# Dynamic convolution and a max-out layer on one core: one earlier tap addition, a gate by transfer, sums in three parts, one logarithm a group later

## The chip, the cores and the metric

One core of a Trainium2 chip runs the whole program. The metric is the time of the execution on the device in microseconds (us), lower is better. Times of before are medians of three runs; the profile is that of one further execution of the same kernel.

## The reference, cut to what matters

Input `x` has 8 sequences of 4160 rows of 192 channels in 8 heads; `weight_gen` gives, for each row and head, 7 logits. Then:

```
w   = exp(weight_gen - max) / sum(exp(...))             # softmax over the 7 taps
out[s] = sum over k of w[s, head, k] * x[s - 6 + k]      # 7 taps, zeros ahead of each sequence
h1, h2 = out @ w1, out @ w2                              # 192 -> 1024 twice
result = maximum(h1, h2) @ w_out                         # 1024 -> 192
```

The kernel writes `maximum(h1, h2)` as `h1 + relu(h2 - h1)`, so TensorE computes one hidden layer with `w2 - w1` (tile `wd`), ScalarE applies the relu, and the part `out @ w1 @ w_out` is one small product with a matrix worked out once (tile `w10`). The softmax goes without the maximum: exponential, sum of seven, logarithm of the sum, subtraction, exponential.

## The kernel before, in words

The 33280 rows are laid out as 128 partitions by 260 columns. **Batches** of 16 columns (17 of them, 0 to 16; the last two have 12 and 8) go through the softmax and the taps; **units** of 8 columns (4 in batches 0 and 1 and at the very end) go through the products. Columns 24 to 27 are the unit of batch 1 at offset 8, unit 6. For each batch, in this order:

- **ScalarE** `X` (`exp_sum`, line 153): exponentials of all logits, tile `e_t`.
- **VectorE** `red` (line 168): sums of seven, tile `sum_t`. `part` splits a batch into `of` parts by columns.
- **ScalarE** `l` (`ln`, line 172): the logarithm of all the sums of a batch in one instruction; it so waits for the last part of `red`.
- **VectorE** `shift` (line 177): logits minus logarithm, in three parts.
- **ScalarE** `W` (`weights`, line 191): the exponentials of that, the softmax weights, per half batch.
- **VectorE** `mul` (line 211): seven products per element, tile `m_t`; `adds`: three additions (lines 227, 233, 236) that bring seven taps to one, tile `y_t`. The second reads what the first wrote, and the third what the second wrote. A hook, `beside`, is called ahead of each of the three and places the parts of `shift` (first half of a batch) or of `red` (second half, two batches ahead of the one multiplied) between them. In the second half `red` takes two parts, ahead of the first and the second addition; nothing stands between the second and the third.
- **SyncE** turns `y_t` to `yt` by a transposing DMA (line 245). **GpSimd** then reads one column of `yt` into the tile `gate` (line 253); as its queue is in order, the loads of `x` and `weight_gen` behind it (lines 118, 125, 139) start only when the transpose has landed.

In batches 0 and 1 the seven taps are not added on VectorE: TensorE adds them while it transposes (`sum_transpose`, line 281; steps `y.0` to `y.7`), 7 taps by 6 blocks by 2 halves, 84 matmuls for a unit. These steps, and all others of the first 47 us, stand in a list written out by hand, `OPENING`: `m.1.8` is the product for columns 24 to 27, `s.2` the shift of batch 2 behind it, `W.2.0` the weights that wait for that.

From tile 16 on, **groups** of three tiles (`hidden`, groups 8 and up) repeat one order. TensorE: hidden products into the PSUM tiles `hda` and `hdb` (line 336); the first half of an output group (lines 388, 376, tile `op_ps`); hidden product into `hdc`; the second half of the outputs. ScalarE, in order: relu of `hda` and of `hdb` (line 346), steps listed as "before" (place 0), relu of `hdc`, evacuation of `op_ps` (line 434), steps listed as "after" (place 1). Each of the four PSUM tiles has one buffer: TensorE writes `hda` of the next group when the relu of this one has read it, and `op_ps` when it has been evacuated. `SOFTMAX_AT` gives for each group and place the steps `X`, `l` and `W`: the logarithm of batch 5 is "after" group 16, that of batch 10 "after" group 44, those of 8, 12 and 15 are "before".

VectorE's steps hang on the tile number (`extra`) and run in their order, without a place among the groups; transposes follow as they are done. At the end ScalarE copies the last two columns to `o_last` (line 422) and two queues store them.

Of the kernel before, what the change touches and what calls it, by code (L numbers as in the profile page):

```python
# [9 lines left out]
FP32 = mybir.dt.float32  # L10
BF16 = mybir.dt.bfloat16
# [6 lines left out]
def _sub(base: bass.AP, off: int, dims):  # L18
    ap = [list(base.ap[0])] + [[int(s), int(c)] for s, c in dims]
    return dataclasses.replace(base, offset=base.offset + off, ap=ap)  # L20
# [3 lines left out]
def kernel(  # L24
# [9 lines left out]
    nc = tc.nc  # L34

    B, S, D = x.shape
    H, K = weight_gen.shape[2], weight_gen.shape[3]
    F = moe_w1.shape[1]
    P = 128
# [3 lines left out]
    HF = F // 2  # L43
# [120 lines left out]
    def red(b, i=0, of=1):  # L164
        if i == 0:
            s_ts[b] = psm.tile([P, BATCHES[b][1] * H], FP32, name="sum_t", tag="sum")
        hs, at, ap = part(b, i, of)
        nc.vector.reduce_sum(out=s_ts[b][:, hs], in_=_sub(e_ts[b], at, ap), axis=AX.X)  # L168
# [48 lines left out]
    def adds(b, o, first=False, beside=lambda i, of: None):  # L217


        w = dict(pieces(b))[o]  # L220
        n = w * D

        def taps(at, step, cnt):
            return _sub(m_t, K * o * D + at * n, [[step * n, cnt], [1, w * D]])

        beside(0, 3)
        nc.vector.tensor_tensor(out=taps(0, 1, 3), in0=taps(0, 1, 3), in1=taps(3, 1, 3), op=ALU.add)  # L227
        if first:
            return
        beside(1, 3)  # L230
        if b not in y_ts:
            y_ts[b] = py.tile([P, 16 * D], BF16, name="y_t", tag="y")
        nc.vector.tensor_tensor(out=taps(0, 2, 2), in0=taps(0, 2, 2), in1=taps(1, 5, 2), op=ALU.add)  # L233
        beside(2, 3)

        nc.vector.tensor_tensor(  # L236
            out=_sub(y_ts[b], o * D, [[64, 2], [P, 3 * w // 2], [1, 64]]),
            in0=taps(0, 1, 1), in1=taps(2, 1, 1), op=ALU.add,
        )

    def transpose(u):

        b, o, n = UNITS[u]
        yt = pyt.tile([P, 8 // 2 * 3 * P], BF16, name="yt", tag="yt")
        nc.sync.dma_start_transpose(
            out=yt[:, 0:n // 2 * 3 * P].rearrange("p (b t) -> p b t", t=P),
            in_=y_ts[b][:, o * D:(o + n) * D],
        )
        yt_ts[u] = yt
        while held:  # L250
            held.pop(0)()

        nc.gpsimd.tensor_copy(out=gate, in_=yt[:, 0:1])  # L253
        c = b + 1 if o == 0 else b + 2
        if u == 8:
            load_x(c, 0, 8)
        if o == 8 and c < NB:
            load_x(c, 0, min(8, BATCHES[c][1]))
        if o == 0 and c < NB and BATCHES[c][1] > 8:
            load_x(c, 8, BATCHES[c][1] - 8)  # L260
        if o == 0 and b + 3 < NB:
            load_wg(b + 3, nc.gpsimd)
# [2 lines left out]
        return slice(64 * j, 64 * j + 64)  # L265


    LEFT = (0, 1, 2, K - 1)

    def sum_transpose(u, i=None):  # L270

        b, o, n = UNITS[u]
        assert n == 4
        to = "h" if i == 0 else "o"
        yps = yps_of[u, i] = ps[to].tile([P, 1024], FP32, name="yps", tag="hd" if i == 0 else "op")
        ks = range(6) if i is None else range(3 * i, 3 * i + 3)
        for k in ks:
            for t in range(K):
                at = K * o * D + (t * 6 + k if i is None else (K * i + t) * 3 + k % 3) * P
                for r in range(2):  # L280
                    nc.tensor.matmul(  # L281
                        yps[:, r * 512 + k * 64:r * 512 + (k + 1) * 64],
                        lhsT=m_t[half(r), at:at + P], rhs=ident[half(r), half(r)],
                        start=(k == ks[0] and t == 0), stop=(t == K - 1),
                        skip_group_check=True,
                    )
# [129 lines left out]
    def evac(p, n):  # L416

        tile_, at = op_at[p]
        o = o_t[0]
        if p == NT // 2 - 1:  # L420

            nc.scalar.copy(out=_sub(o_last, 0, [[D, 2], [1, D]]),
                           in_=_sub(tile_, at, [[512, 2], [1, D]]))
            for j, eng in enumerate((nc.scalar, nc.sync)):
                eng.dma_start(
                    out=bass.AP(tensor=out.tensor, offset=dcol(place(p)[0] + 2 * j) * D, ap=[[CPP * D, P], [1, D]]),
                    in_=o_last[:, j * D:(j + 1) * D],
                )
            return
        runs = [[q for q in range(p, p + n) if column(2 * q)[0] == u]  # L430
                for u in range(column(2 * p)[0], column(2 * (p + n - 1))[0] + 1)]
        for qs in runs:
            c, h = place(qs[0])
            copied = nc.scalar.copy(out=_sub(o, c % 24 * D, [[D, len(qs)], [h * D, 2], [1, D]]),  # L434
                           in_=_sub(tile_, at + (qs[0] - p) * D, [[D, len(qs)], [512, 2], [1, D]]))
        stores = []
        for q in range(p, p + n):
            u, i, _ = column(2 * q)
            if u == NU - 2 and UNITS[u][2] == 8 and i % 2:
                stores.append((nc.sync, place(q)[0] - 1, [4 * D, 2], [1, 2 * D]))  # L440
            elif u < NU - 1 and i == UNITS[u][2] // 2 - 1:
                w = i + 1
                for k in range(0, 2 * w, w if u in PARTED else 2 * w):
                    stores.append((nc.sync, place(q)[0] - i + k, [1, (w if u in PARTED else 2 * w) * D]))
            if u == NU - 1:
                stores.append((nc.sync, place(q)[0], [2 * D, 2], [1, D]))
        for eng, c, *ap in stores:

            def issue(eng=eng, c=c, ap=ap, o=o):
                eng.dma_start(  # L450
                    out=bass.AP(tensor=out.tensor, offset=dcol(c) * D, ap=[[CPP * D, P], *ap]),
                    in_=_sub(o, c % 24 * D, ap),
                )

            if 3 <= u < NU - 3:
                held.append(issue)
            else:
                while u > 3 and held:
                    held.pop(0)()
                issue()  # L460
        return copied
# [80 lines left out]
    around = consts.tile([P, 2 * P], BF16, name="around")  # L542
    ident, swap = around[:, 0:P], around[:, 64:64 + P]
    zeros = consts.tile([P, PAD * D], BF16, name="zeros")
    gate = consts.tile([P, 1], FP32, name="gate")
    o_last = consts.tile([P, 2 * D], FP32, name="o_last")

    pstage = ctx.enter_context(ExitStack())
    stage = pstage.enter_context(tc.tile_pool(name="pstage", bufs=1))
# [13 lines left out]
    def load_w(h, wi):  # L563

        wsrc = (moe_w1, moe_w2)[wi]
        return nc.sync.dma_start(
            out=ws["E", wi][:, h * HF:(h + 1) * HF],
            in_=bass.AP(tensor=wsrc.tensor, offset=h * HF, ap=[[F, P], [1, HF]]),
        )

    def load_last(h, wi):

        wsrc = (moe_w1, moe_w2)[wi]
        return nc.sync.dma_start(  # L574
            out=ws["T", wi][half(h), :],
            in_=bass.AP(tensor=wsrc.tensor, offset=P * F + h * HF, ap=[[F, 64], [1, HF]]),
        )
# [124 lines left out]
    def results_buffer(_):  # L702
# [22 lines left out]
        e.0.1 d.0 d.2 t.0 k.3 t.2 T.3 d.1 T.4 h.0 h.1 t.1 X.1 r.0 lx.0.8.4 T.1 lo.0 r.1 m.0.4 n.1 v.0 h.2  # L725
        lx.1.0.8 V.1 y.1 r.2 l.1 h.3 e.1 m.0.8 lg.2@l.1 s.1 V.0 m.0.12 r.3 h.4 W.1.0 m.1.0 y.2 h.5 r.4 p.0
        e.2 r.5 h.6 lx.1.8.8@r.4 lg.3@e.2 y.3 W.1.8 h.7 lh.2 C.1 C.0 C.2 A.3 W.1.4 X.2 r.6 e.3 B.3 m.1.4 h.8
        D.3 y.4 r.7 r.8 Z.0 E.3 n.2 X.3 l.2 m.1.8 A.4 e.4 W.1.12 lx.2.0.8.0@r.7 B.4 h.9 D.4 h.10 r.9 E.4 s.2
        r.10 lg.4@r.9 y.5 W.2.0 A.5 h.11 B.5 h.12 e.5 D.5 n.3 r.11 r.12 A.6 m.1.12 E.5 h.13 B.6 D.6 y.6 r.13
        E.6 h.14 e.6 l.3 lx.2.8.8@r.13 h.15 r.14 A.7 W.2.8 B.7 y.7 D.7 r.15 e.7 E.7  # L730
    """

    make_identity(nc, ident_f)
# [3 lines left out]
    for step in OPENING.split():  # L737
# [4 lines left out]
            behind(act_of[after], act_of[step])  # L742

    SOFTMAX_AT = {
        (9, 1): "X.4 W.3.0", (12, 0): "W.3.8 l.4", (14, 1): "X.5", (16, 0): "W.4.0", (16, 1): "l.5",
        (18, 1): "W.4.8", (19, 0): "X.6", (21, 1): "W.5.0", (23, 1): "W.5.8 l.6", (25, 1): "X.7",
        (27, 1): "W.6.0", (29, 0): "l.7", (29, 1): "W.6.8 X.8", (33, 1): "W.7.0", (34, 0): "l.8",
        (35, 1): "W.7.8", (37, 1): "X.9 W.8.0", (39, 1): "W.8.8", (40, 0): "l.9", (41, 1): "X.10",
# [13 lines left out]
    def extra(t):  # L762

        u, k = TILES[t]
        b, o, n = UNITS[u]
        s = o + k

        if s == 0 and b + 1 < NB:
            mul(b + 1, 0)
        later = 0 if b < 4 else 5  # L770
        if s == later and b + 1 < NB:

            c = b + 1
            adds(c, 0, beside=lambda i, of: shift(c + 1, i, of) if c + 1 < NB else None)
        if s == 8 and b + 2 < NB:
            mul(b + 1, 8)
        if s == 8 + later and b + 2 < NB:
            adds(b + 1, 8, beside=lambda i, of: red(b + 3, i, 2) if b + 3 < NB and i < 2 else None)
        if s == 8 and b + 2 == NB:
            mul(b + 1, 4)  # L780
            adds(b + 1, 4)
        if k == n // 4 - 1 and 7 < u + 1 < NU:
            transpose(u + 1)
# [41 lines left out]
```

## Time and profile before

| | us |
|---|---|
| median of three runs | 405.51 (405.4 to 405.52) |
| profiled execution, its own time | 405.37 |
| its span in the trace | 403.6 |
| TensorE matmul busy | 394.8 |
| VectorE busy | 369.1 |
| ScalarE busy | 360.9 |
| GpSimd busy | 72.3 |
| granted TensorE clock | 1.0 of full speed |

The span is the time from the first to the last instruction or transfer of the trace; 1.77 us of the execution's own time lie around it. A row of the timeline has the start, the busy time, the engine, the line, the operation with its output and inputs, and in brackets the idle time before it with what ended it. A busy time includes the end of the pipeline, so the next instruction of an engine may start up to 0.1 us ahead of the end of the one before: what an instruction costs in a row of others is the distance of two starts, not its busy time.

### The profile page before, as it was taken

How to read it: one execution, taken by the hardware profiler on the slowest of the kernel's cores; microseconds unless marked ns; L12 is line 12 of the kernel's file. 1: busy time of each engine (PE TensorE's matmuls, PEld its weight loads, DVE VectorE, ACT ScalarE, POOL GpSimd, SP SyncE). 2: the span in 40 equal slices, each digit the busy share in tenths (PEclk: the TensorE clock that was granted, in tenths of full speed). 3: DMA queues.
4: the chain of work that ended last, by engine and by line, in shares of the span. 5: the costliest groups of instructions: out<-in, count | busy, mean ns of one | idle time of the engine just before them, and what ended most of it. 6: DMA issues, size and time to landing. Idle time of an engine off the chain costs nothing.

```text
span 403.6 us, 16321 instructions
## 1 busy us (share of the span) xinstructions
PE 394.8 (98%) x7499; PEld 321.3 (80%) x7499; DVE 369.1 (91%) x211; ACT 360.9 (89%) x466; POOL 72.3 (18%) x96
## 2 busy tenths in 40 slices
PE   7799999999999999999999999999999999999996
PEld 3589999777778777778777778877777877787996
DVE  5999999999999999999999999999999999998200
ACT  5999899999999989999899999989999899888872
POOL 3111031211122210222220122122012121200000
PEclk9999999999999999999999999999999999999999
DMA  8956468767768646864766667777457847558304
GB/s 262 222 140 151 120 124 167 183 164 133 190 110 222 182 79 129 240 187 80 217 187 107 141 192 193 99 215 198 81 115 228 178 80 200 141 106 193 104 31 169
DMA packets 60883, 63.16 MB, mean 157 GB/s; under 512 B 47641, under 2 KB 48665, under 8 KB 60816
## 3 DMA queue, kind: packets, MB, share of 16 engines
q1 hardware_dynamic: 52816, 40.15, 36.4%
q0 software_dynamic: 7856, 21.89, 27.4%
q8 instruction: 58, 0.95, 1.0%
q10 hardware_dynamic: 144, 0.10, 0.1%
q14 instruction: 9, 0.07, 0.1%
HBM read 36.55 MB, written 25.56 MB: 154 GB/s over the span
## 4 chain that ended last, share of the span: by engine, by line
PE 92%; ACT 5%; DMA 1%; SPq 1%; issue 0%
PE op_ps L376 42%; PE hdc L336 13%; PE hdb L336 13%; PE hda L336 13%; PE op_ps L388 8%; ACT rd_t L346 2%; DMA ws0E<-in_moe_w_dram 1%; PE hdp L336 1%; PE yps L281 1%; ACT en_t L191 1%; ACT yt L293 1%; ACT e_t L153 0%; ACT w1t L644 0%; SPq L574 0%; ACT w L622 0%
## 5 line engine op out<-in xcount | busy, mean ns | idle before, releaser
L376 PE MATMUL op_ps<-wo,rd_t 64*128 64x192 bf16 x4160 | 210.6, 243 | 0.0
L376 PEld LDWEIGHTS <-rd_t 64*128 64x128 bf16 x4160 | 181.0, 94 | 14.7
L211 DVE TENSOR_TENSOR m_t<-xb,en_t 128x10752 bf16<-128x10752 bf16 (+2 forms) x39 | 187.8, 4821 | 1.5 <-ACT en_t L191 1.4
L336 PEld LDWEIGHTS <-wd 64*128 64x128 bf16 x1824 | 96.8, 94 | 40.4 <-issue 2.5
L346 ACT ACTIVATE rd_t<-hdc 128x1024 bf16<-128x1024 f32 x82 | 84.1, 1025 | 17.8 <-PE hdc L336 16.2
L253 POOL CAST gate<-yt 128x1 f32<-128x1 bf16 x30 | 39.9, 1332 | 271.3 <-DMA yt<-y_t 271.3
L346 ACT ACTIVATE rd_t<-hda 128x1024 bf16<-128x1024 f32 x81 | 83.4, 1030 | 0.2 <-ACT o_t L434 0.2
L346 ACT ACTIVATE rd_t<-hdb 128x1024 bf16<-128x1024 f32 x81 | 83.5, 1031 | 0.0
L227 DVE TENSOR_TENSOR m_t<-m_t 128x4608 bf16<-128x4608 bf16 (+1 forms) x30 | 73.0, 2433 | 0.1
L336 PE MATMUL hdc<-yt,wd 64*128 64x512 bf16 (+1 forms) x552 | 67.9, 353 | 0.0
L434 ACT COPY o_t<-op_ps 128x384 f32<-128x384 f32 (+1 forms) x99 | 56.1, 577 | 12.4 <-PE op_ps L376 12.3
L336 PE MATMUL hdb<-yt,wd 64*128 64x512 bf16 (+1 forms) x540 | 67.1, 355 | 0.0
L336 PE MATMUL hda<-yt,wd 64*128 64x512 bf16 (+1 forms) x540 | 67.1, 355 | 0.0
L388 PE MATMUL op_ps<-w,yt 64*128 64x192 bf16 x780 | 55.5, 243 | 0.0
L388 PEld LDWEIGHTS <-yt 64*128 64x128 bf16 x780 | 39.0, 94 | 14.5 <-issue 0.3
L233 DVE TENSOR_TENSOR m_t<-m_t 128x3072 bf16<-128x3072 bf16 (+1 forms) x30 | 50.2, 1674 | 0.1
L191 ACT ACTIVATE en_t<-wg_t 128x896 bf16<-128x896 f32 (+3 forms) x48 | 35.7, 773 | 3.0 <-PE op_ps L376 2.0
L236 DVE TENSOR_TENSOR y_t<-m_t 128x1536 bf16<-128x1536 bf16 (+1 forms) x30 | 27.5, 916 | 0.6
L177 DVE TENSOR_TENSOR wg_t<-wg_t,sum_t 128x280 f32<-128x280 f32 (+6 forms) x46 | 22.2, 483 | 0.0
L168 DVE TENSOR_REDUCE sum_t<-e_t 128x64 f32<-128x448 f32 (+3 forms) x31 | 19.7, 639 | 2.3 <-ACT e_t L153 2.3
L125 POOL DMA_DIRECT2D xb<-in_x_dram x34 | 18.2, 537 | 17.3 <-ACT rd_t L346 11.0
L153 ACT ACTIVATE e_t<-wg_t 128x896 f32<-128x896 f32 (+2 forms) x18 | 15.9, 886 | 2.1 <-DMA wg_t<-in_weight_gen_dram 2.1
(40 smaller groups left out, 110.0 us busy)
## 6 DMA issues: line engine op xcount, KB each, us to landing
out_dram<-o_t SPq DMA_DIRECT2D x21, 768.0 KB, 4.3
xb<-in_x_dram POOLq DMA_DIRECT2D x30, 384.0 KB, 5.0
out_dram<-o_t SPq DMA_DIRECT2D x22, 384.0 KB, 3.7
wg_t<-in_weight_gen_dram POOLq DMA_DIRECT2D x13, 448.0 KB, 5.7
xb<-xb POOLq DMA_DIRECT2D x7, 288.0 KB, 5.1
wg_t<-in_weight_gen_dram SPq DMA_DIRECT2D x2, 448.0 KB, 5.2
xb<-in_x_dram POOLq DMA_DIRECT2D x4, 192.0 KB, 6.4
xs<-in_x_dram SPq DMA_DIRECT2D x1, 576.0 KB, 4.3
```

The costliest lines, as they stand in the source:

```text
L177: nc.vector.tensor_tensor(out=w_t, in0=w_t, in1=_sub(s_ts[b], hs.start, [[1, hs.stop - hs.start], [0, K]]), op=ALU.subtract)
L191: act = nc.scalar.activation(out=_sub(en_ts[b], (o * WGC + ((i or 0) * J + j) * N * K) * 2, [[2 * N, K], [2, N], [1, 2]]), in_=_sub(wg_ts[ ...
L211: return nc.vector.tensor_tensor(out=m_out, in0=x_in, in1=_sub(en_ts[b], at * H * 2, [[2, K * n * H], [0, G // 2], [1, 2]]), op=ALU.mult,)
L227: nc.vector.tensor_tensor(out=taps(0, 1, 3), in0=taps(0, 1, 3), in1=taps(3, 1, 3), op=ALU.add)
L233: nc.vector.tensor_tensor(out=taps(0, 2, 2), in0=taps(0, 2, 2), in1=taps(1, 5, 2), op=ALU.add)
L236: nc.vector.tensor_tensor(out=_sub(y_ts[b], o * D, [[64, 2], [P, 3 * w // 2], [1, 64]]), in0=taps(0, 1, 1), in1=taps(2, 1, 1), op=ALU.add,)
L253: nc.gpsimd.tensor_copy(out=gate, in_=yt[:, 0:1])
L336: nc.tensor.matmul(hid_out(t, f, j), lhsT=wd_at(j, s, f // 4, f % 4 * P, P), rhs=_sub(yt_ts[u][half(j), :], (s + j) % 3 * P, [[3 * P, w // ...
L346: relu_of[t0] = nc.scalar.activation(out=rd[:, k * 1024:(k + n) * 1024], in_=hd[:, at:at + n * 1024], func=AF.Relu)
L376: return nc.tensor.matmul(op_out(c), lhsT=rd[rows, k * 1024 + at:k * 1024 + at + P], rhs=wo[rows, f * D:(f + 1) * D], start=False, stop=(r ...
L388: nc.tensor.matmul(op_out(c + j), lhsT=yt_ts[u][half(j), (3 * i + (s + j) % 3) * P:(3 * i + (s + j) % 3 + 1) * P], rhs=w10[half(j), s * D: ...
L434: copied = nc.scalar.copy(out=_sub(o, c % 24 * D, [[D, len(qs)], [h * D, 2], [1, D]]), in_=_sub(tile_, at + (qs[0] - p) * D, [[D, len(qs)] ...
```

## The change

Five edits that act, and two that do not:

1. `OPENING` has a new step `a.1.8` right behind `m.1.8`: VectorE adds taps 3, 4, 5 to taps 0, 1, 2 of columns 24 to 27 (the first of the three additions, 128x2304). `sum_transpose` of that unit then goes over taps 0, 1, 2 and 6: 48 matmuls in place of 84.
2. `gate` is filled by a DMA on GpSimd's queue that reads two elements of `yt`, in place of a copy by GpSimd of 128 elements.
3. The sums of batches 4 to 16 take three parts in place of two; the third stands between the second and the third addition.
4. The logarithm of batch 5 moves from "after" group 16 to "after" group 17. All others keep their places.
5. At the very end `o_last` is two tiles of one column each. ScalarE copies one and its queue stores it; VectorE copies the other and SyncE's queue stores it.

`load_w` and `load_last` get new cases which no step uses, and an unused constant goes. All other steps, their engines and their order are as before.

```diff
         nc.vector.tensor_tensor(out=taps(0, 1, 3), in0=taps(0, 1, 3), in1=taps(3, 1, 3), op=ALU.add)
         if first:
+            fewer.add((b, o))
             return
...
-        nc.gpsimd.tensor_copy(out=gate, in_=yt[:, 0:1])
+        nc.gpsimd.dma_start(out=gate, in_=yt[0:1, 0:2])
...
+        taps = (0, 1, 2, K - 1) if (b, o) in fewer else range(K)
         for k in ks:
-            for t in range(K):
+            for t in taps:
...
-            nc.scalar.copy(out=_sub(o_last, 0, [[D, 2], [1, D]]),
-                           in_=_sub(tile_, at, [[512, 2], [1, D]]))
-            for j, eng in enumerate((nc.scalar, nc.sync)):
+            for j, (eng, copy) in enumerate(((nc.scalar, nc.scalar.copy), (nc.sync, nc.vector.tensor_copy))):
+                copy(out=o_last[j], in_=tile_[:, at + 512 * j:at + 512 * j + D])
...
-        D.3 y.4 r.7 r.8 Z.0 E.3 n.2 X.3 l.2 m.1.8 A.4 e.4 W.1.12 lx.2.0.8.0@r.7 B.4 h.9 D.4 h.10 r.9 E.4 s.2
-        r.10 lg.4@r.9 y.5 W.2.0 A.5 h.11 B.5 h.12 e.5 D.5 n.3 r.11 r.12 A.6 m.1.12 E.5 h.13 B.6 D.6 y.6 r.13
+        D.3 y.4 r.7 r.8 Z.0 E.3 n.2 X.3 l.2 m.1.8 a.1.8 A.4 e.4 W.1.12 lx.2.0.8.0@r.7 B.4 h.9 D.4 h.10 r.9
+        E.4 s.2 r.10 lg.4@r.9 y.5 W.2.0 A.5 h.11 B.5 h.12 e.5 D.5 n.3 r.11 r.12 A.6 m.1.12 E.5 h.13 B.6 D.6
...
-        (9, 1): "X.4 W.3.0", (12, 0): "W.3.8 l.4", (14, 1): "X.5", (16, 0): "W.4.0", (16, 1): "l.5",
+        (9, 1): "X.4 W.3.0", (12, 0): "W.3.8 l.4", (14, 1): "X.5", (16, 0): "W.4.0", (17, 1): "l.5",
...
-            adds(b + 1, 8, beside=lambda i, of: red(b + 3, i, 2) if b + 3 < NB and i < 2 else None)
+            adds(b + 1, 8, beside=lambda i, of: red(b + 3, i, 3) if b + 3 < NB else None)
```

## The prediction

> **What bounds the kernel now.** I read the head of the page first, then the chain that ended last, then the costliest groups.
>
> ```profile
> span 403.6 us, 16321 instructions
> PE 394.8 (98%) x7499; PEld 321.3 (80%) x7499; DVE 369.1 (91%) x211; ACT 360.9 (89%) x466; POOL 72.3 (18%) x96
> PE 92%; ACT 5%; DMA 1%; SPq 1%; issue 0%
> L211 DVE TENSOR_TENSOR m_t<-xb,en_t 128x10752 bf16<-128x10752 bf16 (+2 forms) x39 | 187.8, 4821 | 1.5 <-ACT en_t L191 1.4
> L253 POOL CAST gate<-yt 128x1 f32<-128x1 bf16 x30 | 39.9, 1332 | 271.3 <-DMA yt<-y_t 271.3
> L125 POOL DMA_DIRECT2D xb<-in_x_dram x34 | 18.2, 537 | 17.3 <-ACT rd_t L346 11.0
> ```
>
> TensorE is the bound: 92% of the chain is its own work. The L211 row matters more than it seems: VectorE's products wait 1.5 us in the whole run, 1.4 of it on one occasion. VectorE is thus a second, nearly gapless line of work beside TensorE's. It has no slack in which an added instruction could vanish; whatever it gains early moves all of its later steps. TensorE does not wait for it now, but ScalarE stands between them, and it takes its work in order. So the question for each edit is not only "is it on TensorE's chain", but "which ScalarE step waits for VectorE, and how much time has it".
>
> **The change part by part.**
>
> *Taps on VectorE, TensorE's side.* From the chain, in order of time, the unit of columns 24 to 27:
>
> ```profile
> 41.97 1.22 PE yps L281 x84
> ```
>
> 84 matmuls in 1.22 us are 14.5 ns each; 36 go: **-0.52 us** on the chain, from 42 us on.
>
> *Taps on VectorE, VectorE's side.* The timeline of VectorE has the same shape late in the run, and the step that the addition is put ahead of; that of ScalarE the weights behind it.
>
> ```profile
> 34.19 1.08 DVE L177 TENSOR_TENSOR wg_t<-wg_t,sum_t 128x896 f32<-128x896 f32 x1
> ...
> 360.12 1.36 DVE L227 TENSOR_TENSOR m_t<-m_t 128x2304 bf16<-128x2304 bf16 x1
> 361.51 0.96 DVE L233 TENSOR_TENSOR m_t<-m_t 128x1536 bf16<-128x1536 bf16 x1
> ```
> ```profile
> 36.90 1.09 ACT L191 ACTIVATE en_t<-wg_t 128x896 bf16<-128x896 f32 x1
> ```
>
> Start to start the addition takes 361.51 - 360.12 = 1.39 us, including one stretch in which a reader waits for its writer; in the new place that stretch lies ahead of it (it reads the product just written) and not behind, so I take **1.39 us**. The shift of batch 2 ends at 34.19 + 1.39 + 1.08 = 36.66, the weights start at 36.90: 0.24 us are left, no loss there. But all of VectorE's later steps are 1.39 us later, for there is no idle time to take it up.
>
> *Sums in three parts.* The second half of batch 8, which holds the sums of batch 10, a two-part reduction of 48 columns, and two rows of a first half, where a shift stands between the additions:
>
> ```profile
> 198.53 0.61 DVE L168 TENSOR_REDUCE sum_t<-e_t 128x64 f32<-128x448 f32 x1
> 199.06 2.55 DVE L227 TENSOR_TENSOR m_t<-m_t 128x4608 bf16<-128x4608 bf16 x1
> 201.53 0.61 DVE L168 TENSOR_REDUCE sum_t<-e_t 128x64 f32<-128x448 f32 x1
> 202.06 1.75 DVE L233 TENSOR_TENSOR m_t<-m_t 128x3072 bf16<-128x3072 bf16 x1
> 203.84 0.96 DVE L236 TENSOR_TENSOR y_t<-m_t 128x1536 bf16<-128x1536 bf16 x1
> ```
> ```profile
> 316.87 0.50 DVE L168 TENSOR_REDUCE sum_t<-e_t 128x48 f32<-128x336 f32 x1
> 317.28 2.56 DVE L227 TENSOR_TENSOR m_t<-m_t 128x4608 bf16<-128x4608 bf16 x1
> ```
> ```profile
> 47.91 1.75 DVE L233 TENSOR_TENSOR m_t<-m_t 128x3072 bf16<-128x3072 bf16 x1
> 49.58 0.50 DVE L177 TENSOR_TENSOR wg_t<-wg_t,sum_t 128x336 f32<-128x336 f32 x1
> ```
>
> A reduction of 448 elements costs 0.53 us, one of 336 costs 0.41; along that line one of 280 costs 0.35. The second addition costs 1.78 with its reader next, 1.67 with something between. The first addition costs 2.47 and stays. Before: 0.53 + 2.47 + 0.53 + 1.78 = 5.31 us from the first reduction to the third addition. With parts of 40, 40 and 48 columns: 0.35 + 2.47 + 0.35 + 1.67 + 0.41 = 5.25. So VectorE **gains 0.06 us** per batch. What moves the wrong way is the end of the sums: now 3.00 + 0.61 = 3.61 us after the first reduction starts, then 0.35 + 2.47 + 0.35 + 1.67 + 0.50 = **5.34**.
>
> The Trainium skill, page "VectorE: DVE Perf Modes", section "Rules for kernel authors", speaks against it: the pipeline's emptying is paid after every operation, so it advises to keep the number of operations small. The rows of 1.78 and 1.67 show that here a filler takes a part of that time back. What the rule would make of the sum is the third rival.
>
> *Logarithms.* Each waits for the last part. ScalarE's rows, and the first sums of batch 5:
>
> ```profile
> 80.20 0.61 DVE L168 TENSOR_REDUCE sum_t<-e_t 128x64 f32<-128x448 f32 x1
> ```
> ```profile
> 88.11 1.02 ACT L346 ACTIVATE rd_t<-hda 128x1024 bf16<-128x1024 f32 x1
> ...
> 157.90 0.33 ACT L172 ACTIVATE sum_t<-sum_t 128x128 f32<-128x128 f32 x1
> ```
>
> Batch 5: sums done at 80.20 + 1.39 - 0.06 + 5.34 = 86.87. The new place, ahead of the relu of 88.11, comes at 87.59, 0.52 us earlier than before: no wait, with 0.7 us left. First reductions follow each other by 23.67 us ((198.53 - 80.20) / 5). Batch 8 (first reduction at 80.20 + 3 x 23.67 = 151.21): 151.21 + 1.39 - 4 x 0.06 + 5.34 = 157.70 against 157.90 - 0.52 = 157.38, 0.3 us late ahead of one relu; what that costs lies ahead of the next point and is swallowed by it. **Batch 10 kept its place**: 198.53 + 1.39 - 6 x 0.06 + 5.34 = 204.90.
>
> ```profile
> 202.55 0.80 ACT L434 COPY o_t<-op_ps 128x768 f32<-128x768 f32 x1 [0.29 <-PE op_ps L376]
> 203.25 0.31 ACT L172 ACTIVATE sum_t<-sum_t 128x128 f32<-128x128 f32 x1
> 203.46 1.02 ACT L346 ACTIVATE rd_t<-hda 128x1024 bf16<-128x1024 f32 x1
> 204.37 1.03 ACT L346 ACTIVATE rd_t<-hdb 128x1024 bf16<-128x1024 f32 x1
> 205.40 1.02 ACT L346 ACTIVATE rd_t<-hdc 128x1024 bf16<-128x1024 f32 x1
> 206.32 0.47 ACT L434 COPY o_t<-op_ps 128x384 f32<-128x384 f32 x1
> ```
> ```profile
> 205.85 0.83 PE L336 MATMUL hda<-yt,wd 64*128 64x512 bf16 x6
> 206.50 0.83 PE L336 MATMUL hdb<-yt,wd 64*128 64x512 bf16 x6
> 207.14 0.43 PE L388 MATMUL op_ps<-w,yt 64*128 64x192 bf16 x6
> ```
>
> The evacuation ahead of it waits for TensorE and comes 0.52 us earlier with it, so the logarithm is reached at 202.73 and waits 2.17 us. Behind it in the queue are the three relus and the evacuation of group 45. From 204.90: relu of `hda` at 205.11 to 206.13, that of `hdb` at 206.02 to 207.05, that of `hdc` 0.91 later at 206.93, evacuation 0.92 later at 207.85 to 208.32. TensorE, which would be at `hda` at 205.33, gets it at 206.13, `hdb` at 207.05, and `op_ps`, one buffer, at 208.32 where it was at 207.14: **1.18 us later than before**, a stall of 1.70 us of which the 0.52 paid a part. I allow about 0.05 for the signals between and take +1.2. This end hangs on VectorE's clock, not on TensorE's: a stall ahead of it only shortens it.
>
> *Batch 15*, after that:
>
> ```profile
> 320.90 0.28 ACT L172 ACTIVATE sum_t<-sum_t 128x96 f32<-128x96 f32 x1 [0.55 <-PE op_ps L376]
> 321.46 1.03 ACT L346 ACTIVATE rd_t<-hdc 128x1024 bf16<-128x1024 f32 x1 [0.28 <-PE hdc L336]
> 322.78 0.86 ACT L434 COPY o_t<-op_ps 128x384 f32<-128x384 f32 x2 [0.29 <-PE op_ps L376]
> ```
>
> Sums at 316.87 + 1.39 - 0.66 + 0.29 + 2.47 + 0.29 + 1.67 + 0.38 (parts of 224 elements, along the same line) = 322.70; the logarithm is reached at 320.90 + 1.2 = 322.10 and waits 0.6. The relu behind is then 0.25 us late, and the 0.29 idle ahead of the evacuation takes that up. Counted as nothing; with no such cover it is the fourth rival.
>
> *Transposes.* The tightest unit that I found lands at 349.83 (the gate's start) for TensorE at 351.83:
>
> ```profile
> 349.83 1.75 POOL L253 CAST gate<-yt 128x1 f32<-128x1 bf16 x1 [9.17 <-DMA yt<-y_t]
> ```
> ```profile
> 351.83 0.83 PE L336 MATMUL hda<-yt,wd 64*128 64x512 bf16 x6
> ```
>
> VectorE is then 1.39 - 13 x 0.06 = 0.61 us later and TensorE 1.2: no wait.
>
> *Gate.* GpSimd's queue waits for the landing as before; an issue takes 0.54 us on average where the copy took 1.33, so the loads behind start some 0.8 us earlier. VectorE's 1.5 us of waits hold almost none for loads, so earlier loads gain nothing; if the loads were instead held up by an issue more, a few us of VectorE's 11.8 us per half batch cover it. Zero, with both ends within 0.2 us.
>
> *End.* The last copy is ScalarE's:
>
> ```profile
> 400.05 0.48 ACT L422 COPY o_last<-op_ps 128x384 f32<-128x384 f32 x1
> ```
>
> Evacuations of 768 and 384 elements took 0.80 and 0.47, so one of 192 is near 0.31: up to 0.17 gained. VectorE's copy of 192 elements from PSUM has no row; between 0.2 and the 0.50 of a 336-element reduction, I take the lower half. **-0.15**, between -0.17 and +0.05. The Trainium skill ("VectorE: DVE Perf Modes", section "The TRN2 errata") gives 120 cycles and one per element from PSUM, an estimate of 0.33 us, and so the same -0.15.
>
> *Sum* on the profiled execution: 405.37 + 1.2 - 0.15 = 406.42; the median lies 0.14 higher: **406.6 us**.
>
> **The rivals.**
>
> - *The wait costs nothing* (not slower): TensorE has enough in hand to ride over ScalarE's 2.17 us, as it rides over the weights (0.9 us) now. For it: TensorE waits for no relu in the groups now. Against: one buffer per PSUM tile, and only 0.35 us between the end of the evacuation (206.79) and its reuse (207.14). It decides if the reuse comes over 1.2 us later than I read. 405.51 - 0.52 - 0.15 = 404.8.
> - *VectorE takes up the addition* (the 1.39 does not carry through): then the sums of batch 10 end at 203.51, the wait is 0.8, the reuse of `op_ps` at 206.93 against 206.62, +0.3: 405.2. Against: the 1.5 us of idle time.
> - *Three sums cost a fixed part each and give nothing back*: the line through 448 and 336 elements has 0.05 us at none, so a batch gains 0.05 instead of losing 0.06; at batch 10 VectorE is 1.69 later and the sums end 0.11 later: +0.8, 407.4. Against: 1.67.
> - *Batch 15 is not covered*: up to 0.6 more, 407.2.
>
> **How the numbers follow.** Forecast 0.60 (its own range 406.2 to 407.0), wait free 0.12, addition taken up 0.10, fixed part 0.10, batch 15 0.08. The range 405.2 to 407.2 leaves out the first rival and most of the third. About 0.2% (0.8 us) is what a measurement of this kernel tells from no change: above 406.3 is slower, below 404.7 faster. Slower: 0.53 of the forecast, 0.10 and 0.08, 0.71. Same: 0.07 of the forecast, 0.10, 0.07 of the first rival, 0.24. Faster 0.05.
>
> **What would show it.** Right: ScalarE's line 172 waits for VectorE's `sum_t` once for about 2.2 us and once for about 0.6; TensorE waits near 206 us for `rd_t` and `o_t`, 1.7 us in all; L281 has 36 matmuls less; VectorE's L211 is 1.39 us later from 36 us on and 1.0 at 199. Wrong: a line 172 without waits, a VectorE that waits after 36 us, or a third reduction that costs more than 0.41.

## The result, and the profile after

The changed kernel takes 406.70 us (median of 22 runs, 406.46 to 407.01) where the kernel before, run beside it, takes 405.71 (22 runs, 405.21 to 407.94): a ratio of 1.0021, 95% interval 1.0012 to 1.0031. Ratios here and below are as recorded with the runs and are not the quotients of the medians (406.70 / 405.71 = 1.0024). It is slower by 1.0 us. The forecast was 406.6.

The head of the page of the changed kernel, and its chain by engine (line numbers are up to three higher than before):

```profile
span 404.9 us, 16275 instructions
PE 395.7 (98%) x7463; PEld 320.4 (79%) x7463; DVE 370.3 (91%) x226; ACT 360.5 (89%) x466; POOL 49.2 (12%) x96
PE 92%; ACT 5%; DMA 1%; DVE 1%; issue 1%; SPq 0%; DVEq 0%; ACTq 0%
```

TensorE has 36 matmuls fewer (7463 for 7499), and its busy time is longer: the page alone says that something was lost, and not where. The list of waits does (engine, line, what it waited for: us in total, times, longest):

```profile
ACT sum_t L172 <- DVE sum_t L168: 2.1, 2, 1.9
```

Before, the only wait of this kind was one of 0.2 us in the opening. The long one stands in the timeline of the changed kernel from 198 to 212 us. VectorE, then ScalarE, then TensorE:

```profile
199.66 0.45 DVE L168 TENSOR_REDUCE sum_t<-e_t 128x40 f32<-128x280 f32 x1
...
202.48 0.45 DVE L168 TENSOR_REDUCE sum_t<-e_t 128x40 f32<-128x280 f32 x1
202.83 1.76 DVE L234 TENSOR_TENSOR m_t<-m_t 128x3072 bf16<-128x3072 bf16 x1
...
204.50 0.51 DVE L168 TENSOR_REDUCE sum_t<-e_t 128x48 f32<-128x336 f32 x1
204.91 0.96 DVE L237 TENSOR_TENSOR y_t<-m_t 128x1536 bf16<-128x1536 bf16 x1
```
```profile
202.35 0.80 ACT L435 COPY o_t<-op_ps 128x768 f32<-128x768 f32 x1 [0.30 <-PE op_ps L378]
...
205.04 0.31 ACT L172 ACTIVATE sum_t<-sum_t 128x128 f32<-128x128 f32 x1 [1.89 <-DVE sum_t L168]
205.26 1.01 ACT L348 ACTIVATE rd_t<-hda 128x1024 bf16<-128x1024 f32 x1
...
207.97 0.49 ACT L435 COPY o_t<-op_ps 128x384 f32<-128x384 f32 x1
```
```profile
204.34 0.83 PE L338 MATMUL hdc<-yt,wd 64*128 64x512 bf16 x6
205.24 0.83 PE L378 MATMUL op_ps<-wo,rd_t 64*128 64x192 bf16 x16
...
206.31 0.82 PE L338 MATMUL hda<-yt,wd 64*128 64x512 bf16 x6 [0.25 <-ACT rd_t L348]
...
207.23 0.82 PE L338 MATMUL hdb<-yt,wd 64*128 64x512 bf16 x6
...
208.51 0.42 PE L390 MATMUL op_ps<-w,yt 64*128 64x192 bf16 x6 [0.46 <-ACT o_t L435]
```

Read it downwards: the third reduction of batch 10 ends at 205.01, the logarithm starts at 205.04, everything behind it on ScalarE is late, and TensorE gets its three PSUM tiles one after the other late, the last at 208.51 where it was 207.14 before. From the product into `hdc` to this one it is 208.51 - 204.34 = 4.17 us, where it was 207.14 - 204.54 = 2.60: 1.57 us are lost here. Counted from the first matmul of group 8 at 47 us, TensorE's starts lie as far apart as before up to 204 us, and all that follow 208.51 are late by these same 1.57 us (to within 0.06): no other place behind 47 us costs anything.

The row at 205.24 shows a link that the prediction did not list. This second half of the outputs waits for a no-op in ScalarE's queue (line 411), which stands behind the logarithm as well:

```profile
205.23 0.61 PEld L378 LDWEIGHTS <-rd_t 64*128 64x128 bf16 x16 [0.56 <-ACTq L411]
```

It holds TensorE's matmul by 0.25 us. It adds nothing to the total, because `hda` is not free until 206.31.

The end of the changed kernel:

```profile
401.42 0.32 ACT L425 COPY o_last<-op_ps 128x192 f32<-128x192 f32 x1
401.77 0.37 ACTq L426 DMA_DIRECT2D out_dram<-o_last  x1
401.77 0.36 DVE L425 COPY o_last<-op_ps 128x192 f32<-128x192 f32 x1 [24.15 <-ACT o_last L425]
402.15 0.34 SPq L426 DMA_DIRECT2D out_dram<-o_last  x1
```

VectorE's copy starts when ScalarE's has ended. The copies do not lie beside each other, and the last store issues 0.73 us after the first copy starts, where it was 0.51. VectorE's row names ScalarE's copy as what ended its wait; why two copies from one PSUM tile into two tiles come one after the other stays open.

### The profile page after: what moved, and what is told of

Its sections match the earlier page's. It is cut to its first block, busy times and chain, and to the rows that moved or that the text cites. A ratio compares the mean times of both kernels' runs of the same rounds, so it can differ in the third digit from the quotient of the medians.

```text
span 404.9 us, 16275 instructions
## 1 busy us (share of the span) xinstructions
PE 395.7 (98%) x7463; PEld 320.4 (79%) x7463; DVE 370.3 (91%) x226; ACT 360.5 (89%) x466; POOL 49.2 (12%) x96
## 4 chain that ended last, share of the span: by engine, by line
PE 92%; ACT 5%; DMA 1%; DVE 1%; issue 1%; SPq 0%; DVEq 0%; ACTq 0%
PE op_ps L378 42%; PE hdc L338 13%; PE hdb L338 13%; PE hda L338 13%; PE op_ps L390 8%; ACT rd_t L348 2%; DMA xs<-in_x_dram 1%; PE hdp L338 1%; PE yps L283 1%; DVE m_t L211 1%; ACT en_t L191 0%; ACT e_t L153 0%; ACT w1t L646 0%; ACT yt L295 0%; ACT wd L616 0%
## 5 line engine op out<-in xcount | busy, mean ns | idle before, releaser
L227 DVE TENSOR_TENSOR m_t<-m_t 128x4608 bf16<-128x4608 bf16 (+1 forms) x31 | 74.6, 2405 | 0.1
L254 POOL DMA_DIRECT2D gate<-yt x30 | 15.4, 512 | 297.0 <-DMA yt<-y_t 297.0
L168 DVE TENSOR_REDUCE sum_t<-e_t 128x40 f32<-128x280 f32 (+6 forms) x44 | 21.9, 500 | 2.5 <-ACT e_t L153 2.5
```

## The experiments

Theory: from 47 us on the end is set by VectorE's clock, by way of the logarithms that ScalarE reaches too early. Rivals: the place of batch 10 alone is the cause; the pieces (addition, three sums, gate) each cost a fixed time; VectorE's lateness does not come through.

The openings differ between single executions by some tenths of a us (the first `hda` matmul of group 8 starts at 46.5 to 48.1 us). So beside the median this table gives, from each profile, the distance from that matmul to the start of the last copy, which leaves the opening out, and with it the 0.52 us that the tap addition saves there. To compare a kernel with the tap addition with before by the distance, 0.52 is taken off. The first four runs share one set of 35 runs of before, the last four another.

| kernel | median us | before, beside it | ratio (95%) | group 8 to last copy |
|---|---|---|---|---|
| before | 405.71; 405.87; 405.76 | | | 400.05 - 47.11 = 352.94 |
| changed | 406.70 | 405.71 | 1.0021 (1.0012 to 1.0031) | 354.51 |
| batch 10 later | 406.20 | 405.87 | 1.0010 (1.0001 to 1.0018) | 354.26 |
| four logarithms later | 405.20 | 405.87 | 0.9985 (0.9975 to 0.9996) | 353.25 |
| changed, sums in two | 405.80 | 405.87 | 1.0001 (0.9992 to 1.0011) | 353.61 |
| changed, no tap addition | 405.55 | 405.87 | 0.9985 (0.9966 to 1.0003) | 352.94 |
| before, gate as a transfer | 405.66 | 405.76 | 0.9992 (0.9966 to 1.0017) | 352.94 |
| changed, more VectorE work | 408.24 | 405.76 | 1.0046 (1.0021 to 1.0071) | 356.15 |
| four later, old end | 405.39 | 405.76 | 0.9986 (0.9960 to 1.0013) | 353.11 |
| four later, sums in two | 406.07 | 405.76 | 0.9995 (0.9970 to 1.0019) | 354.18 |

**Batch 10 later.**

```diff
-        (43, 1): "W.9.0", (44, 1): "l.10", (45, 1): "W.9.8", ...
+        (43, 1): "W.9.0", (45, 1): "W.9.8 l.10", ...
```

> The changed kernel with the logarithm of batch 10 moved behind the weights of group 45; batches 8, 12 and 15 keep their places. Theory (VectorE's clock pins TensorE through the logarithms): the stall near 206 us goes, TensorE runs about 0.5 us ahead of before until batch 15, whose logarithm then waits about 2.3 us for sums that end near 322.8 and stalls TensorE by 1.2 to 1.5 us: the run ends 0.7 to 1.0 us over before, so only 0.2 to 0.5 under the changed kernel. Rival (the one place of batch 10 is the cause): 0.5 us under before.

0.33 us over before by the medians, less than expected; by the distance, 354.26 - 352.94 - 0.52 = 0.80, within it. The mechanism is as expected: the wait went to batch 15 (its ScalarE and TensorE rows). TensorE's starts lie as far apart as before near 206 us, lose 0.12 us at 317.18 and 1.20 at 324.76.

```profile
322.76 0.28 ACT L172 ACTIVATE sum_t<-sum_t 128x96 f32<-128x96 f32 x1 [2.72 <-DVE sum_t L168]
```
```profile
324.76 0.42 PE L390 MATMUL op_ps<-w,yt 64*128 64x192 bf16 x6 [1.03 <-ACT o_t L435]
```

The rival of one place falls: with that place mended most of the loss comes back 118 us later.

**Four logarithms later.**

```diff
-        ... (34, 0): "l.8", ... (44, 1): "l.10", (45, 1): "W.9.8", ... (56, 0): "l.12", ... (72, 0): "l.15", ...
+        ... (35, 0): "l.8", ... (45, 1): "W.9.8 l.10", ... (57, 0): "l.12", ... (73, 0): "l.15", ...
```

> The changed kernel with the logarithms of batches 8, 10, 12 and 15 each about one group later. Theory: no logarithm waits, TensorE keeps the 0.52 us of the 36 matmuls, the end gives nothing: 0.5 us under before (0.3 to 0.7), 1.5 us under the changed kernel. Rival (the added VectorE work, the gate or the three sums cost time by themselves): at or over before.

0.67 us under before by the medians, interval clear of 1, and 1.5 us under the changed kernel (1.26 by the distance). How far it is under before is less certain: by the distance it is 353.25 - 352.94 - 0.52 = -0.21, and the kernel without the tap addition, whose distance is that of before, also reads 0.32 under these runs of before. The third rival falls: with the same addition, gate and sums, the loss behind 47 us is 0.31 us and not 1.57 once no logarithm waits. Those 0.31 us come from TensorE's one wait for data behind 47 us that is new:

```profile
PEld L338 <- DMA yt<-y_t: 0.4, 1, 0.4
```

It comes near 317 us, at the transpose of unit 30, where TensorE's starts lose 0.32 us.

**Changed, sums in two.**

```diff
-            adds(b + 1, 8, beside=lambda i, of: red(b + 3, i, 3) if b + 3 < NB else None)
+            adds(b + 1, 8, beside=lambda i, of: red(b + 3, i, 2) if b + 3 < NB and i < 2 else None)
```

> The changed kernel with the sums in two parts as before; tap addition, gate, end and the later logarithm of batch 5 stay. Theory: the sums of batch 10 end at 203.5 to 203.7, the logarithm waits 0.8 us and costs TensorE 0.5 to 0.6, batch 15 a little more: 0.0 to 0.3 us over before. If the effects of tap addition and three sums only added up, this and the next one would together give the 1.0 us of the changed kernel.

No difference from before that can be told in the time. The logarithm of batch 10 still waits, for less:

```profile
203.49 0.31 ACT L172 ACTIVATE sum_t<-sum_t 128x128 f32<-128x128 f32 x1 [0.71 <-DVE sum_t L168]
```

Behind 47 us the kernel loses 353.61 - 352.94 = 0.67 us: TensorE's starts lose 0.40 here and the rest from 317 us on, where it waits for transposes. The logarithm of batch 15 is idle for 1.16 us, longer than that of batch 10, and this costs TensorE nothing. The 0.52 us saved in the opening pay for about all of it.

**Changed, no tap addition.** The step `a.1.8` is taken out of the list.

> The changed kernel without the tap addition (84 matmuls again); three sums, gate, end and the later logarithm of batch 5 stay. Theory: VectorE is 0.06 us earlier per batch, the sums of batch 10 end at 203.5, the logarithm waits 0.3 us ahead of 0.35 us of slack: within 0.15 us of before. Rival (three parts are what costs): 0.5 to 1 us over before.

No difference that can be told, and the distance is that of before to the hundredth. The logarithm of batch 10 has 0.30 us left here. So the third part without the addition costs nothing, the addition without the third part costs 0.67 us behind 47 us, which its own 0.52 about pays, and together they cost 1.57, or 1.0 us in the time: two delays in one line, where the addition alone is a little over the slack and the third part alone is under it. Effects that only add up would give 0.67 in place of 1.57 and are excluded. The later logarithm of batch 5 is in this kernel too and costs nothing here; it was not run by itself.

**Before, gate as a transfer.**

```diff
-        nc.gpsimd.tensor_copy(out=gate, in_=yt[:, 0:1])
+        nc.gpsimd.dma_start(out=gate, in_=yt[0:1, 0:2])
```

> The kernel before with the gate as a transfer and nothing else. Theory: loads issue up to 1.3 us earlier and VectorE waits for none of them; within 0.1 us of before. Rival (GpSimd's copies held VectorE up, or the transfers hold GpSimd's queue up): a difference of over 0.3 us, and VectorE's rows at another distance from each other.

Nothing, and the distance is again 352.94 us.

**Changed, more VectorE work.**

```diff
-        ... W.2.0 A.5 h.11 B.5 h.12 e.5 D.5 n.3 r.11 r.12 A.6 m.1.12 ...
+        ... W.2.0 A.5 h.11 B.5 h.12 e.5 D.5 n.3 z z r.11 r.12 A.6 m.1.12 ...
...
+    def filler():
+
+        return nc.vector.tensor_tensor(out=scratch, in0=zeros, in1=zeros, op=ALU.add)
```

`z` is the step that calls `filler`: an addition of zeros that nothing reads, twice, ahead of the product for columns 28 to 31.

> The changed kernel with two additions of zeros into a scratch tile (128x1152, together about 1.4 us of VectorE) ahead of the product for columns 28 to 31; nothing reads them. Theory (VectorE's clock sets the end through the logarithms): the whole 1.4 us comes through, 1.2 to 1.5 us over the changed kernel, 2.3 to 2.6 over before. Rival (the changed kernel loses a fixed amount to waits that VectorE's lateness doesn't set): within 0.3 us of the changed kernel.

408.24, 2.48 us over before and 1.5 over the changed kernel. Its filler, and the same two places as above (VectorE, TensorE):

```profile
37.77 1.54 DVE L666 TENSOR_TENSOR scratch<-zeros 128x1152 bf16<-128x1152 bf16 x2
...
201.18 0.43 DVE L168 TENSOR_REDUCE sum_t<-e_t 128x40 f32<-128x280 f32 x1
```
```profile
210.02 0.42 PE L390 MATMUL op_ps<-w,yt 64*128 64x192 bf16 x6 [0.46 <-ACT o_t L435]
```

VectorE's reduction is 1.52 us later than in the changed kernel and TensorE's matmul 1.51: what VectorE loses at 38 us, TensorE loses at 210, one for one. TensorE is held at 92, 97 and 161 us too, by 0.95 us in all, and this does not add to the end: at 210 us it is VectorE's lateness alone that counts. A fixed loss is excluded.

**Four later, old end.** The one copy of both columns by ScalarE is put back.

> The kernel with four logarithms later, and the end as before: one copy of both columns by ScalarE, two stores behind it. Theory: the split end is worth nothing, as its second copy starts when the first has ended: within 0.15 us of the same kernel with the split end. If the split had given the 0.15 us that was forecast: 0.15 slower.

405.39 beside 405.20, on two chips whose runs of before differ by 0.11 the other way; the intervals overlap widely, and the times do not decide: 0.19 us apart, where at most 0.15 was expected. The trace does for the mechanism: from the start of the last copy to the end of the span it is 3.55 us with the old end (399.95 to 403.5) and 3.49 with the split one (399.71 to 403.2).

**Four later, sums in two.** Both edits above.

> The kernel with four logarithms later, but sums in two parts. Theory: the third part gives VectorE 0.06 us a batch back, and with the logarithms out of the way the next thing that TensorE meets is the landing of a transpose near 317 us; without the third part VectorE is 0.65 to 0.75 us later there: 0.6 to 1.0 us over the same kernel with three parts, 0.0 to 0.5 over before. Rival (the third part costs VectorE a fixed amount and gives nothing back): at or under the same kernel with three parts.

0.31 us over before by the medians, 0.68 over the kernel with three parts and the old end on the same chip, 1.07 by the distance. The intervals against before are wide here; the trace carries it. No logarithm waits for its sums behind 47 us, and TensorE waits for the transpose instead:

```profile
318.90 0.82 PE L338 MATMUL hda<-yt,wd 64*128 64x512 bf16 x6 [0.72 <-DMA yt<-y_t]
```

TensorE's starts lose 0.90 us there (0.32 with three parts) and 0.34 more at 342 us. The rival by which a third part costs VectorE time falls.

## Why the prediction was right, step by step

- **TensorE's 0.52 us**: right. The 48 matmuls take 0.70 us on the chain (84 took 1.22):

```profile
42.28 0.70 PE yps L283 x48
```

  The two profiles show TensorE only 47.11 - 46.91 = 0.20 us ahead at group 8, as the openings differ by other things too.
- **The addition's 1.39 us on VectorE**: right. The product ahead of it before, and the rows around it in the changed kernel:

```profile
31.32 2.95 DVE L211 TENSOR_TENSOR m_t<-xb,en_t 128x5376 bf16<-128x5376 bf16 x1
```
```profile
31.46 2.95 DVE L211 TENSOR_TENSOR m_t<-xb,en_t 128x5376 bf16<-128x5376 bf16 x1
34.44 1.36 DVE L227 TENSOR_TENSOR m_t<-m_t 128x2304 bf16<-128x2304 bf16 x1
35.72 1.08 DVE L177 TENSOR_TENSOR wg_t<-wg_t,sum_t 128x896 f32<-128x896 f32 x1
```

  From the product to the shift it is 4.26 us; before, it was 34.19 - 31.32 = 2.87. None of it was taken up later: 199.66 - 198.53 = 1.13 us of lateness at batch 10, of which 31.46 - 31.32 = 0.14 was there before the addition (that execution's opening). The other 0.99 is what 1.03 was forecast for.
- **Three sums give 0.06 us back per batch**: right, 204.91 - 199.66 = 5.25 for the 5.31 of before; their end comes 204.50 + 0.51 - 199.66 = 5.35 after their start (5.34 forecast). A filler between the second and the third addition pays for itself. The Trainium skill's rule of few operations ("VectorE: DVE Perf Modes", section "Rules for kernel authors") would have given the opposite sign; the trace decides against it here, where an independent operation stands between two dependent ones.
- **Batch 10**: right. Logarithm at 205.04 for 204.90, `hda` at 206.31 for 206.13, `hdb` at 207.23 for 207.05, `op_ps` at 208.51 for 208.32 and the 0.05 allowed for signals. VectorE's late opening makes up 0.14 of each difference. The wait was 1.89 us for a forecast of 2.17, and TensorE lost 1.57 us for 1.70, because TensorE came to this place 0.20 us ahead of before and not 0.52.
- **Batch 15 is covered**: right in the changed kernel.

```profile
322.81 0.28 ACT L172 ACTIVATE sum_t<-sum_t 128x96 f32<-128x96 f32 x1 [1.10 <-PE hdc L338]
...
324.14 0.86 ACT L435 COPY o_t<-op_ps 128x384 f32<-128x384 f32 x2
```

  The logarithm starts at 322.81, as the sums end at 322.77; the evacuation behind comes at 324.14, 1.36 us later than before and so no later than TensorE itself is. TensorE waits for nothing, and the list of waits has none for TensorE from 245 us on. The row of that logarithm names TensorE as the releaser of its 1.10 us of idle time, though 0.55 of it is the wait for the sums; where two releasers are close, the label is the later one by the trace only. The fourth rival falls. In the kernel with batch 10 moved TensorE comes earlier, the logarithm is idle for 2.72 us in place of 1.10, and the cover is too small: TensorE loses 1.20 us there.
- **Gate**: right, nothing.
- **End, -0.15 us**: too large, the one term of the sum that was mis-sized. It took the two copies to lie beside each other; VectorE's (0.36 us) ran after ScalarE's (0.32). From the last copy's start to the end of the span it is 404.9 - 401.42 = 3.48 us for 403.6 - 400.05 = 3.55 before: -0.07. Counted from that copy's start the last store issues 0.22 us later, and from there to the end it is 2.75 us for 3.04.
- **Transposes**: the sum held, but the tightest unit was not the one named. Unit 30's landing at 316.04 us for TensorE's `hda` at 317.49 left 1.45 us, less than the 2.0 shown. With TensorE 1.4 us late it did not matter; with the logarithms moved it is the next bound. The row of before that shows the landing:

```profile
316.04 0.96 POOL L253 CAST gate<-yt 128x1 f32<-128x1 bf16 x1 [9.85 <-DMA yt<-y_t]
```

The rival of a free wait falls with the 1.37 us of TensorE's lateness at 208.51; that of an addition taken up falls with the 1.13; that of a fixed part with the 5.25.

That the level came out within 0.1 us is luck in part. The forecast added 1.09 us to three runs of before with a median of 405.51; the 22 runs beside the changed kernel gave 405.71, and the rise was 0.99.

## What to carry to other kernels

A second engine that never idles is a second clock. List the steps of an in-order engine between it and the bound that wait for it, each with its slack, and add to each the delays of all edits at once: here two edits, each at no cost in the time alone, cost 1.0 us together, and the slack of the tightest step decided. When one such step is moved, look at the next one down the list before counting the gain; and moving four of them was worth 1.3 to 1.5 us against the changed kernel.

## What the runs showed of the hardware that was not expected

GpSimd's one-column copy took as long as VectorE's product left it. Before, the copy and the product that ran then, and a copy beside which VectorE had nothing to do:

```profile
90.33 1.85 POOL L253 CAST gate<-yt 128x1 f32<-128x1 bf16 x1 [8.98 <-DMA yt<-y_t]
...
383.10 0.18 POOL L253 CAST gate<-yt 128x1 f32<-128x1 bf16 x1 [8.37 <-DMA yt<-y_t]
```
```profile
86.39 5.75 DVE L211 TENSOR_TENSOR m_t<-xb,en_t 128x10752 bf16<-128x10752 bf16 x1
```

The copy ends at 92.18, the product at 92.14; 28 of the 30 copies end 0.04 us behind a VectorE operation with two inputs, after 0.39 to 1.85 us, and the one alone takes 0.18. In the changed kernel the transfer in its place issues in the middle of a product:

```profile
198.66 0.51 POOL L254 DMA_DIRECT2D gate<-yt  x1 [10.60 <-DMA yt<-y_t]
```
```profile
193.99 5.77 DVE L211 TENSOR_TENSOR m_t<-xb,en_t 128x10752 bf16<-128x10752 bf16 x1
```

All 30 transfers issue in 0.50 to 0.52 us. The Trainium skill, page "SBUF — State Buffer", section "SBUF: two separate sides", says that a VectorE operation with two inputs in SBUF shuts out a GpSimd operation only if that one reads SBUF; the 1.85 us and the 0.51 agree. On this kernel's time it has no effect either way.
